# A new order of steps: four heads at a time, three level/angle buffers, six buffers of transposed tiles

## The chip, the cores and the metric

The kernel runs on one core of one Trainium2 chip. The metric is the device time of one execution in microseconds (us). Three runs of the kernel before gave 346.86 us as their median (345.96 to 346.95).

## The reference

All tensors are float32. B = 4 batches, H = 8 heads, S = 768 time steps, D = 48 channels of a head; the model width is 8 x 48 = 384. First a recurrence with a complex decay, whose real part is read out, then a gated convolution:

```python
mag = np.sqrt(a_re * a_re + a_im * a_im)
scale = np.minimum(mag, 0.999) / (mag + 1e-06)
a_re_n, a_im_n = (a_re * scale, a_im * scale)
for t in range(S):
    ar, ai = (a_re_n[:, :, t, :, None], a_im_n[:, :, t, :, None])
    new_re = ar * S_re - ai * S_im
    new_im = ar * S_im + ai * S_re
    kv = np.einsum('bhd,bhe->bhde', k[:, :, t], v[:, :, t])
    S_re, S_im = (new_re + kv, new_im)
    y[:, :, t] = np.einsum('bhd,bhde->bhe', q[:, :, t], S_re)
...
x = y.transpose(0, 2, 1, 3).reshape(B, S, H * D)
for k in range(5):
    gate_pre += conv_w[k][None, None, :] * xp[:, k:k + S, :]    # xp: x with four zero rows ahead
gate = 1.0 / (1.0 + np.exp(-gate_pre))
val = x @ w_val
out = gate * val @ w_out
```

## The kernel before

The recurrence is not stepped through. Logarithms of the decay's size (the level) and its angle are summed up along time; keys and queries are multiplied by the exponentials of the level, falling or rising, and by the cosine and sine of the angle, so that causal products of 96-wide rows (48 cosine and 48 sine parts) give what the recurrence gives. This is done in chunks of 128 time steps with a state that is carried between chunks on TensorE.

**Units.** `UNITS` (line 22) cuts the work into nine units u0 to u8, each (batch, first head, heads, half of the time, halves). u0 has two heads of batch 0, first half; u1 the other six; u2 is batch 0, second half, all eight heads; u3 and u4 are the halves of batch 1, u5 and u6 of batch 2, u7 and u8 of batch 3. A half has three chunks of 128 steps. A unit's heads are taken in groups of two pairs, four heads (line 85; u0 has one group of two heads, u1 a group of four and one of two). `chunks` (lines 86 to 92) lists (unit, chunk, group): with `GROUPWISE = False` each chunk runs through its groups before the next chunk comes, with `True` each group runs through the three chunks of the half before the next group comes. The generators for scores, masks, states, state copies, outputs and output copies all go by this list.

**Steps.** `ORDER` (lines 31 to 44) is one string; each letter advances one generator by one step (table `streams`, lines 772 to 783; loop 784 to 785). Every step's instructions on TensorE, DVE and ACT are tied to the one before on the same engine by `turn` (line 114), so the string fixes the order on these three engines. SyncE issues the DMAs; its queue is not tied by `turn` (`PIN_SP = False`), the DMAs stand in it as they are emitted. The letters:

- A loads the inputs of a unit (`load`, 149); V loads a batch's v, and then in a step of its own moves the first 64 rows of each chunk, for all heads of a unit, to the lower and upper half of `v_lo` (`load_vl`, 182), a single constant tile; L and w load and convert the weights.
- a to p make level and angle of a unit in the tile `main` (`p_ln`, 344, takes the buffer): a logarithm and exponential on ACT; b, g, h, i, k, m on DVE; c, d, e, f on both; j and l a small product on TensorE (335) for the sum over the 128 partitions; n and o absolute value and sines on ACT into `qx`; p two exponentials on ACT.
- q makes the keys `kx` on DVE (two products, lines 448 and 450), r the queries in `qx` (the same lines). `kx` has one buffer.
- N moves a chunk of keys by DMA from `kx` to `kn` (`move_keys`, 190; lines 201 to 206), where rows are time steps.
- T flips a head's keys or queries: three transposes on TensorE (500) into a PSUM tile `mm`; U copies it on ACT to a tile `kT` or `qT` (508), each of the two kinds with `BUFS['kT']` buffers. Flips go group by group: four heads of keys, then the same four of queries.
- s scores (530) into one of two PSUM tiles; M masks them on DVE (542) into `sm`; t adds keys times values into the one state in PSUM, `S_ps` (564); u copies the four heads' part of it on ACT (579) to `S_sb`, or `S_cr` when the next half needs it; y outputs (601 from the state of the chunk before, 606 and 611 from `sm` with v and `v_lo`); v copies them on ACT (622) to `y_sb`; X collects rows of `y_sb` by DMA into `xT` (646).
- C and D are the two sides of the convolution on DVE (first tap 657, four more 660), G the gate's sigmoid on ACT (679), P values on TensorE (691), Z gate times value on DVE (715), O projections on TensorE (698), Q row copies on ACT to `ot` (728), W stores (734). E is a guard that checks sums for overflow.

**Waits.** Besides the fixed order an instruction waits for its data and for its buffer: a tile of a pool with n buffers can be written when the tile n earlier has been read for the last time. `BUFS` (line 26) holds these counts.

**Tables.** ACT's functions lie in three sets (line 49). `act` (132 to 136) puts a table load (134) ahead of an instruction whose sets do not hold the one loaded last; so the count of loads follows from the order of the letters alone.

Of the kernel before, what the change touches and what calls it, by code (L numbers as in the profile page):

```python
# [21 lines left out]
UNITS = ((0, 0, 2, 0, 1), (0, 1, 6, 0, 1), (0, 0, 8, 1, 1), (1, 0, 8, 0, 1), (1, 0, 8, 1, 1), (2, 0, 8, 0, 1), (2, 0, 8, 1, 1), (3, 0, 8, 0, 1), (3, 0, 8, 1, 1))  # L22
PIECES = ((0, 0, 384), (0, 384, 384), (1, 0, 384), (1, 384, 384), (2, 0, 384), (2, 384, 384), (3, 0, 384), (3, 384, 384))
CONVS = ((0, 0, 384), (0, 384, 384), (1, 0, 384), (1, 384, 384), (2, 0, 384), (2, 384, 384), (3, 0, 384), (3, 384, 384))
GROUPWISE = False
BUFS = {'in': 4, 'v': 2, 'kn': 2, 'xT': 2, 'z': 3, 'main': 2, 'tmp': 1, 'qx': 2, 'kx': 1, 'kT': 9, 'S': 1, 'S_sb': 2, 'S_cr': 4, 'y_sb': 4, 'sm': 2, 'ot': 2, 'mm': 4}
YSLOTS = 2
XSTEP = 2
PIN_SP = False
POOLQ = ''  # L30
ORDER = (
    "AAaaAVbccAaeLfAagLiLiblVmdchwAhwjVdkkwhnwohowjwwwkpkpqcrqAnrTwwNaTeTUwfTUgUNUasiiMlbyomsvsoMNwcMwdwA"
    "htphAjAuqpVyckAVtvkuwyrqAtnvurTNwaTNUTwUTeaTNTbfUwUTUTUTgUTUTUTUisUUicwlMscmysvwXMowysdMMXoshAetvAwt"
    "hsuwuypyMtMtpqjvkAvfrkAuuyqnyvtvXtuurTgaTNTTUiUNTUiTUClUCUNTamTTXtUtbUTUTXuTUCXTUTCUATUTACUtUDsUCusD"
    "cCtDPcCDCPDGCGZGMdZyMhyvesvshMjMoykoyksvvsnMPMuuoyoZyvXOvXpOXQqpOWqXQfWAQWDTrNDTUTrUDTNUTCTUDTUTCUTU"
    "NDTUTDUTCAUTUDVTUTCUTDUVtUCtUDsuuaDtMtsgaAsPbGiAGPGZciMdlZymyvsvhPMhpMyZpqyvsrqvAusAucttujurNMTaTkTN"
    "UyUkUTvMTNnTeTAyUUUTvTUTUTUXTUTUTUTUXTUtUtUsuXuatMtyfbsvsgOAXMoiMcCyiQDlCvWdDymosshvDuOhDCpDjCOQkpWk"
    "cPrqnCPAQqWAGPGZNZrToCNTMTCUyMoNCyevsUvUCXuMtCXyGutZvVtuTTUVTUTUTXTUTUTUTUXTUTUTUTUtUsUsMyMfsyMvsvga"
    "yMsAviuyaMiyDvbulvXtmctAsuXDpOCDCupqOQrqcWAOQAWrNDTQTCUTWTUDTUNDTUCTUTDUTUCTNUTDUTUMTUDTUTUDTaeytAUt"
    "UsUvsuMXuatMyXbyvftsAvgsPMGMGCGDcyZDyvCuDsvCusdMDydMDyvCXhPvCVCGhGhXjZPhkcXejXPZfkknOkZOnDDQDWODQWDD"  # L40
    "gPQWDCoPZDoCDPoDCoCPCCCPCGGZZCOiGGZZiOQiWilQlWmOmpOQqpWqOpQpWOqNQWETrQNTrrUTTUTUTUWTUTNUTUTUTUTUTUTU"
    "TUTUsUqUtsutturTNMTMUTTNTyyvNsvsMtMyyvusvusMUUTMUTUTTyyUUUTUTTUTUTUTUTUsUUtMvsvXusMXysMvXsttuXyuyMvC"
    "sMvDtCtuDyuCDyvMtDvEuXEDyCXPvCCCXGCPGZXCCPZGDDCPDZDCODDGZDOQCWDCODQCWDGGPQWPZZOOQWOQWQW"
)
TURN = 2.0 ** 24
RADIAN = 2.0 * PI / 2.0 ** 32 * (1.0 - 2.0 ** -22)
# [6 lines left out]
def kernel(  # L53
# [34 lines left out]
        for rs, n in (  # L88
            [(rs, n) for rs in groups[u] for n in range(f0 * HN, (f0 + nf) * HN)] if GROUPWISE
            else [(rs, n) for n in range(f0 * HN, (f0 + nf) * HN) for rs in groups[u]]  # L90
# [53 lines left out]
    def dma(key, **kw):  # L144
        pool = key in POOLQ
        ins = (nc.gpsimd if pool else nc.sync).dma_start(**kw)  # L146
        return turn("sp", ins) if PIN_SP and not pool else ins

    def load(u, nm):
        b, h0, g, f0, nf = units[u]  # L150
        t = sb.tile([P, g, nf, JH, D], F32, name=f"{nm}_in", tag="in", bufs=BUFS["in"])
        src = {"ar": a_re, "ai": a_im, "k": k, "q": q}[nm][b, :, f0 * HS:(f0 + nf) * HS]
# [11 lines left out]
    def load_v(u):  # L164
        b, h0, g, f0, nf = units[u]
        if h0 == 0:
            v_b[b] = sb.tile([C, H, NCH, D], F32, name="v_in", bufs=BUFS["v"])
        for hs in halves_of(u):
# [5 lines left out]
    def halves_of(u):  # L174
        b, h0, g, f0, nf = units[u]
        if g == H:
            return [slice(0, H)]
        return [slice(w * (H // 2) + h0, w * (H // 2) + h0 + g // 2) for w in range(2)]
# [11 lines left out]
    def move_keys(u, n):  # L190
        b, h0, g, f0, nf = units[u]
        if n % HN == 0:
            tl[u]["kn"] = sb.tile([C, HN, g * C2 + 32], F32, name="kn", bufs=BUFS["kn"])
            nc.gpsimd.memset(tl[u]["kn"][:, :, g * C2:], 0.0)
# [15 lines left out]
    def load_raw(src):  # L210
        raw = sb.tile([P, NT * (EXT + S)], F32, name="raw", tag="xT", bufs=BUFS["xT"])
        raws.append(raw[:, :NT * DM * 2].bitcast(I64))
        dma("L",
            out=raws[-1].rearrange("p (c o) -> p c o", c=NT), in_=src.rearrange("(c p) o -> p c o", p=P)
        )

    def load_cw():
        raws.append(sb.tile([TAPS * NT, P], I64, name="raw_cw", tag="ot", bufs=BUFS["ot"]))
        dma("L", out=raws[-1], in_=conv_w.rearrange("t (c p) -> (t c) p", p=P))
# [44 lines left out]
    def mm():  # L264
        return ps.tile([P, 512], F32, name="mm", bufs=BUFS["mm"])

# [669 lines left out]
```

## Time and profile before

| | |
|---|---|
| median of three runs | 346.86 us (345.96 to 346.95) |
| the profiled execution | 347.51 us |
| its span, first to last instruction | 345.7 us |
| mean granted TensorE clock, share of full speed | 0.959 |
| instructions | 8663 |

The profile is one execution. Busy time of an engine counts its instructions; a share of the span says nothing of which engine is late at a given time, so the sections on the chain of waits, the timelines and the windows are read beside it. Times are microseconds from the start of the span; "idle before" is how long an engine stood still ahead of an instruction and what ended that. DVE is VectorE, ACT is ScalarE, PE is TensorE, SPq is SyncE's DMA queue. L500 is line 500 of the kernel before.

### The profile page before, as it was taken

The numbers are of one execution on the slowest core, as the hardware profiler recorded it, in microseconds if no ns is written. First come the engines' busy times: TensorE is split into PE (matmuls) and PEld (weight loads), VectorE is DVE, ScalarE is ACT, GpSimd is POOL, SyncE is SP. The second block draws the span as 40 slices with busy tenths as digits, with TensorE's granted clock in tenths as the row PEclk, the third lists the DMA queues.
The fourth block names the chain that finished last, engine by engine and source line by source line (L and its number), as shares of the span: only waits on it lengthen the run. The fifth ranks groups of instructions, "written<-read, shape, count | busy, mean of one in ns | idle before, by whom it ended". The sixth has DMA issues, their size and how long they took to land.

```text
span 345.7 us, 8663 instructions
## 1 busy us (share of the span) xinstructions
PE 278.2 (80%) x3591; PEld 212.4 (61%) x3591; DVE 251.0 (73%) x349; ACT 234.0 (68%) x423; POOL 6.2 (2%) x30
## 2 busy tenths in 40 slices
PE   0375676669994698798979979899999887999993
PEld 0153565558672586586749965777555577896551
DVE  4798979996925977927995179969998946148920
ACT  6989689768783596588974967868595751824121
POOL 5000000000000000000000000000000000000000
PEclk9999999889999699989995999999999999999999
DMA  7995997456017876764074947763311343221112
GB/s 196 354 227 164 234 219 200 132 138 176 24 43 141 241 195 138 203 168 130 31 204 127 193 118 212 232 179 76 91 43 46 108 122 99 44 72 40 52 50 73
DMA packets 58184, 47.83 MB, mean 138 GB/s; under 512 B 9758, under 2 KB 53803, under 8 KB 58139
## 3 DMA queue, kind: packets, MB, share of 16 engines
q1 hardware_dynamic: 58138, 47.21, 53.6%
q8 instruction: 30, 0.49, 0.6%
q14 instruction: 16, 0.12, 0.1%
HBM read 25.97 MB, written 4.72 MB: 89 GB/s over the span
## 4 chain that ended last, share of the span: by engine, by line
PE 47%; DVE 21%; ACT 11%; issue 8%; DMA 7%; SPq 4%; DVEq 0%; ACTq 0%
PE mm L698 10%; PE mm L691 9%; PE mm L500 8%; PE sc_ps L530 5%; SPq L146 4%; PE y_ps L601 4%; DVE z L660 4%; DVE kx L450 4%; PE S_ps L564 3%; ACT main L136 3%; DVE qx L450 3%; PE mm L335 3%; PE y_ps L611 3%; PE y_ps L606 3%; DMA ar_in<-in_a_re_dram 2%
## 5 line engine op out<-in xcount | busy, mean ns | idle before, releaser
L660 DVE SCALAR_TENSOR_TENSOR z<-xT,cw_sb,z 128x384 f32<-128x384 f32 x96 | 55.2, 612 | 0.8
L542 DVE TENSOR_TENSOR sm<-sc_ps,mask 128x384 f32<-128x384 f32 (+1 forms) x51 | 26.6, 530 | 39.3 <-PE sc_ps L530 33.3
L691 PE MATMUL mm<-xT,w_sb 128*128 128x384 f32 x144 | 49.4, 492 | 0.3 <-DMA xT<-y_sb 0.3
L698 PE MATMUL mm<-w_sb,z 128*128 128x384 f32 x144 | 48.5, 489 | 0.0
L530 PE MATMUL sc_ps<-qT,kT 96*64 96x64 f32 x1152 | 43.4, 230 | 3.3 <-ACT qT L139 1.4
L530 PEld LDWEIGHTS sc_ps<-qT,kT 96*64 96x64 f32 x1152 | 39.6, 144 | 5.5 <-issue 2.5
L500 PE MATMUL mm<-ident,kx 128*96 128x128 f32 x192 | 29.0, 302 | 15.3 <-DVE kx L450 9.2
L500 PE MATMUL mm<-ident,qx 128*96 128x128 f32 x192 | 31.0, 317 | 11.6 <-DVE qx L450 6.3
L139 ACT COPY y_sb<-y_ps 112x256 f32<-112x256 f32 (+1 forms) x51 | 17.1, 364 | 33.6 <-PE y_ps L611 33.6
L136 ACT ACTIVATE main<-main 128x1152 f32<-128x1152 f32 (+2 forms) x36 | 38.1, 1061 | 0.6 <-DVE main L419 0.3
L698 PEld LDWEIGHTS mm<-w_sb,z 128*128 128x128 f32 x144 | 27.0, 190 | 18.3
L691 PEld LDWEIGHTS mm<-xT,w_sb 128*128 128x128 f32 x144 | 26.7, 190 | 18.3 <-DMA xT<-y_sb 0.8
L500 PEld LDWEIGHTS mm<-ident,kx 128*96 128x96 f32 x192 | 23.1, 140 | 19.8 <-issue 7.4
L500 PEld LDWEIGHTS mm<-ident,qx 128*96 128x96 f32 x192 | 24.1, 145 | 16.4 <-ACT kT L139 9.5
L139 ACT COPY qT<-mm 96x384 f32<-96x384 f32 x64 | 27.3, 507 | 7.0 <-PE mm L500 6.0
L134 ACT ACT_TABLE_LOAD x24 | 30.8, 1283 | 1.2 <-PEq L920 0.8
L139 ACT COPY ot<-mm 128x384 f32<-128x384 f32 x24 | 11.4, 475 | 27.1 <-PE mm L698 17.2
L139 ACT COPY kT<-mm 96x384 f32<-96x384 f32 x64 | 26.9, 490 | 3.0 <-PE mm L500 2.9
L601 PE MATMUL y_ps<-qT,S_sb 96*48 96x128 f32 x256 | 23.4, 303 | 6.6 <-ACT S_sb L139 4.8
L564 PE MATMUL S_ps<-v_in,kn 128*64 128x48 f32 x640 | 26.4, 236 | 0.9 <-DMA kn<-kx 0.5
L606 PE MATMUL y_ps<-sm,v_in 128*48 128x64 f32 x384 | 21.9, 235 | 5.5 <-DVE sm L542 5.5
L564 PEld LDWEIGHTS S_ps<-v_in,kn 128*64 128x64 f32 x640 | 23.9, 153 | 3.2 <-ACT S_sb L139 1.2
(75 smaller groups left out, 394.2 us busy)
## 6 DMA issues: line engine op xcount, KB each, us to landing
kn<-kx SPq DMA_DIRECT2D x21, 378.0 KB
out_dram<-ot SPq DMA_DIRECT2D x24, 192.0 KB
ar_in<-in_a_re_dram SPq DMA_DIRECT2D x7, 576.0 KB
ai_in<-in_a_im_dram SPq DMA_DIRECT2D x7, 576.0 KB
k_in<-in_k_dram SPq DMA_DIRECT2D x7, 576.0 KB
q_in<-in_q_dram SPq DMA_DIRECT2D x7, 576.0 KB
xT<-y_sb SPq DMA_DIRECT2D x48, 72.0 KB
v_lo<-v_in SPq DMA_DIRECT2D x6, 288.0 KB
```

The source lines that it names most:

```text
L134: turn("act", nc.scalar.preload_act_table_set(sets[0]))
L136: return turn("act", nc.scalar.activation(*args, **kw))
L139: return turn("act", nc.scalar.copy(out, in_))
L500: pe(nc.tensor.transpose(pt[:C2, j, :], src[:, j, f, h, :], ident))
L530: pe(nc.tensor.matmul(o[w * HC:(w + 1) * HC, c * HC:(c + 1) * HC], part(u, 0, h, n, key, key + HC), part(u, 1, h, n, query, query + HC), s ...
L542: dve(nc.vector.tensor_tensor(out=t, in0=sc_ps[i % 2][:, :len(rs) * 3 * HC].rearrange("p (r x) -> p r x", x=3 * HC), in1=mask[:, None, :]. ...
L564: pe(nc.tensor.matmul(S_ps[b][c:c + 64, head(u, h) * D:(head(u, h) + 1) * D], kn[:, n % HN, at:at + 64], v_b[b][:, head(u, h), n], start=( ...
L601: pe(nc.tensor.matmul(to(r, w, 0, C), S_of[b, head(u, h), n - 1], part(u, 1, h, n), start=(r == 0), stop=False, skip_group_check=True,))
L606: pe(nc.tensor.matmul(to(r, w, HC, C), v_b[b][:, head(u, h), n], sm[:, r, (1 + w) * HC:(2 + w) * HC], start=(n == 0 and r == 0), stop=Fals ...
L660: dve(nc.vector.scalar_tensor_tensor(out=z, in0=xT[:, c, EXT + t0 - t:EXT + t0 - t + n], scalar=cw_sb[:, TAPS - 1 - t, c:c + 1], in1=z, op ...
L691: pe(nc.tensor.matmul(pv[:, :n], wv_sb[:, ci, c * P:(c + 1) * P], xT[:, ci, EXT + t0:EXT + t0 + n], start=(ci == 0), stop=(ci == NT - 1),))
L698: pe(nc.tensor.matmul(po[:, :DM], z[:, ci, m:m + P], wo_sb[:, ci, :], start=(ci == 0), stop=(ci == NT - 1)))
```

## The change

`GROUPWISE` becomes `True`: a group of four heads goes through the three chunks of its half before the next group starts. `BUFS` has three level/angle tiles `main` (two before), six transposed tiles of each kind (nine), three `S_sb` (two) and three `y_sb` (four). `ORDER` is replaced as a whole. It holds the same letters as often as before, so the same steps are done; by the rule of lines 132 to 136 it gives 28 table loads where the old one gives 24.

```diff
--- before.py
+++ after.py
@@ -22,25 +22,25 @@
 UNITS = ((0, 0, 2, 0, 1), (0, 1, 6, 0, 1), (0, 0, 8, 1, 1), (1, 0, 8, 0, 1), (1, 0, 8, 1, 1), (2, 0, 8, 0, 1), (2, 0, 8, 1, 1), (3, 0, 8, 0, 1), (3, 0, 8, 1, 1))
 PIECES = ((0, 0, 384), (0, 384, 384), (1, 0, 384), (1, 384, 384), (2, 0, 384), (2, 384, 384), (3, 0, 384), (3, 384, 384))
 CONVS = ((0, 0, 384), (0, 384, 384), (1, 0, 384), (1, 384, 384), (2, 0, 384), (2, 384, 384), (3, 0, 384), (3, 384, 384))
-GROUPWISE = False
-BUFS = {'in': 4, 'v': 2, 'kn': 2, 'xT': 2, 'z': 3, 'main': 2, 'tmp': 1, 'qx': 2, 'kx': 1, 'kT': 9, 'S': 1, 'S_sb': 2, 'S_cr': 4, 'y_sb': 4, 'sm': 2, 'ot': 2, 'mm': 4}
+GROUPWISE = True
+BUFS = {'in': 4, 'v': 2, 'kn': 2, 'xT': 2, 'z': 3, 'main': 3, 'tmp': 1, 'qx': 2, 'kx': 1, 'kT': 6, 'S': 1, 'S_sb': 3, 'S_cr': 4, 'y_sb': 3, 'sm': 2, 'ot': 2, 'mm': 4}
 YSLOTS = 2
 XSTEP = 2
 PIN_SP = False
 POOLQ = ''
 ORDER = (
-    "AAaaAVbccAaeLfAagLiLiblVmdchwAhwjVdkkwhnwohowjwwwkpkpqcrqAnrTwwNaTeTUwfTUgUNUasiiMlbyomsvsoMNwcMwdwA"
-    "htphAjAuqpVyckAVtvkuwyrqAtnvurTNwaTNUTwUTeaTNTbfUwUTUTUTgUTUTUTUisUUicwlMscmysvwXMowysdMMXoshAetvAwt"
-    "hsuwuypyMtMtpqjvkAvfrkAuuyqnyvtvXtuurTgaTNTTUiUNTUiTUClUCUNTamTTXtUtbUTUTXuTUCXTUTCUATUTACUtUDsUCusD"
-    "cCtDPcCDCPDGCGZGMdZyMhyvesvshMjMoykoyksvvsnMPMuuoyoZyvXOvXpOXQqpOWqXQfWAQWDTrNDTUTrUDTNUTCTUDTUTCUTU"
-    "NDTUTDUTCAUTUDVTUTCUTDUVtUCtUDsuuaDtMtsgaAsPbGiAGPGZciMdlZymyvsvhPMhpMyZpqyvsrqvAusAucttujurNMTaTkTN"
-    "UyUkUTvMTNnTeTAyUUUTvTUTUTUXTUTUTUTUXTUtUtUsuXuatMtyfbsvsgOAXMoiMcCyiQDlCvWdDymosshvDuOhDCpDjCOQkpWk"
-    "cPrqnCPAQqWAGPGZNZrToCNTMTCUyMoNCyevsUvUCXuMtCXyGutZvVtuTTUVTUTUTXTUTUTUTUXTUTUTUTUtUsUsMyMfsyMvsvga"
-    "yMsAviuyaMiyDvbulvXtmctAsuXDpOCDCupqOQrqcWAOQAWrNDTQTCUTWTUDTUNDTUCTUTDUTUCTNUTDUTUMTUDTUTUDTaeytAUt"
-    "UsUvsuMXuatMyXbyvftsAvgsPMGMGCGDcyZDyvCuDsvCusdMDydMDyvCXhPvCVCGhGhXjZPhkcXejXPZfkknOkZOnDDQDWODQWDD"
-    "gPQWDCoPZDoCDPoDCoCPCCCPCGGZZCOiGGZZiOQiWilQlWmOmpOQqpWqOpQpWOqNQWETrQNTrrUTTUTUTUWTUTNUTUTUTUTUTUTU"
-    "TUTUsUqUtsutturTNMTMUTTNTyyvNsvsMtMyyvusvusMUUTMUTUTTyyUUUTUTTUTUTUTUTUsUUtMvsvXusMXysMvXsttuXyuyMvC"
-    "sMvDtCtuDyuCDyvMtDvEuXEDyCXPvCCCXGCPGZXCCPZGDDCPDZDCODDGZDOQCWDCODQCWDGGPQWPZZOOQWOQWQW"
+    "AAaaALbcAcLaeLfAagVwiwiwbldmAchwhwjdkwhwhwkjwwnowokcwpkqneAaqwfTNTUNgaiUNipblVtmcVrucwtAuArtwAeTuTUw"
+    "fUgssVidiVMolhMhojmwsakyyvaMkywvnbvpXXwpqcrAcqAAAedTNTUNhTorTUUNUhoTwjUwTTfkTUUgTUpTTiTsUiUksUUMtnMs"
+    "qsplqAyuatyvuvtmaNtTTNMTUTUMrsUsUyNuuwbtAyAvMvMXuycrttyvuXuvtctwTXuTuUTeTUTUTUTUXTfssMUagtAsyaMiyMUi"
+    "UTvCTvCTUTUDPCuDCdDPCoCDCyoDCUhUPCvhXCbXGjGGsZcZsMldMZsmOhpkOQqpWhOAQqcWjQyWrNyvMNTvrTUTUyNUvtVkukXn"
+    "tueTXTUTUTkVfTTAtAUtgUTUATUTUiTuTuisDCsMotCsMoCyyDMUUCTUTDUlCvvPDunmoDtDyuDoDUDUPDvXXGPGZGZsZpsMOMaq"
+    "pOqAQpWOQrpWNrasNyyQvWTvMTNUTqUTUTATUATUbTUTTycAAtvUXUTUTUTquTXcssttMNdMsruyUUyhUUMNvrTvTuTTtyaCNDUC"
+    "UTADUTUACTvTDaXsCsDXuCtDuCtMCsGMyGCUUCTUTMUTCvTbyGyveAutUVtUhUjVUvTukXTuTsksXfMtMsagyyUMUUiTvTiUTvPu"
+    "acPZbnctZyDuDUCUDPvCXDeXdlsZomsoOMMDDOQCWDCDfOCDQphWsDhyQqpjWPMAvkPqGGGPZNZkTNTZUTUrTUONUnrAAOQAWgoT"
+    "TTiQyUiWUyvolTvmTUXUtUsucsXMtMdsyuhyMvCyvDCtvDTuXCTUTDUTXCUTTUDTUPCUUDCCPGCGZCCPpZhpqjOckqsQWstGMuTN"
+    "ZsUMNykryvNTvMTUrTUOUnOQeWfTTTtQgyUWUuTUViTUTiUTUTlvXTmsosXMtMosyDUyDUMUTvDTvTCUPDuCDDpPCDCpDyqtUtDU"
+    "vPquXuXsGDsNMtZyMuNsCvyEGMGNZtvyZurEvTTXUETrUTUOUXTQCTUTWDUTDUTTUDTUTUDTTDsCsMCtyMuCyvCCsGCGtMUtUCTU"
+    "TUCPvCuuGyZtUPUvuXXPZsZsMyMyvsvOMyQWOvXOXQWDOQDWDDPQDWDGDPDZDDPCCCOCCGGOZQZWOQWOQWOQWQW"
 )
 TURN = 2.0 ** 24
 RADIAN = 2.0 * PI / 2.0 ** 32 * (1.0 - 2.0 ** -22)
```

## Rows read from the trace of the kernel before

**Rows 1.** Page, part 1: busy us, share of span, instructions of each engine

```profile
PE 278.2 (80%) x3591; PEld 212.4 (61%) x3591; DVE 251.0 (73%) x349; ACT 234.0 (68%) x423; POOL 6.2 (2%) x30
```

**Rows 2.** Page, part 4: the chain that ended last, by engine

```profile
PE 47%; DVE 21%; ACT 11%; issue 8%; DMA 7%; SPq 4%; DVEq 0%; ACTq 0%
```

**Rows 3.** Windows: us; busy PE, PEld, DVE, ACT, POOL (instructions); PEclk, DMA share, GB/s

```profile
0.00:286.15 286.15, 227.15 (x2845) 173.43 (x2845) 223.45 (x299) 214.58 (x374) 6.22 (x30) 0.95 0.61 154
286.15:345.70 59.55, 51.06 (x746) 39.02 (x746) 27.57 (x50) 19.44 (x49) 0.00 (x0) 0.99 0.23 62
```

**Rows 4.** Timeline, DVE: start, us, line, out<-in, count, [idle before <-what ended it]

```profile
82.56 0.42 DVE L657 TENSOR_SCALAR z<-xT,cw_sb 128x384 f32<-128x384 f32 x1 [2.91 <-DMA xT<-y_sb]
...
103.67 1.36 DVE L448 TENSOR_TENSOR main<-main,k_in 128x1152 f32<-128x1152 f32 x1 [4.63 <-ACT main L136]
...
111.66 0.42 DVE L657 TENSOR_SCALAR z<-xT,cw_sb 128x384 f32<-128x384 f32 x1 [4.04 <-DMA xT<-y_sb]
...
155.60 0.56 DVE L542 TENSOR_TENSOR sm<-sc_ps,mask 128x384 f32<-128x384 f32 x1 [6.67 <-PE sc_ps L530]
...
196.73 1.26 DVE L542 TENSOR_TENSOR sm<-sc_ps,mask 128x384 f32<-128x384 f32 x2 [8.39 <-PE sc_ps L530]
...
283.56 2.56 DVE L450 TENSOR_TENSOR kx<-qx,main 128x2304 f32<-128x2304 f32 x1 [4.57 <-DMA kn<-kx]
```

**Rows 5.** Page, part 5: a group's count, busy us and mean ns

```profile
L134 ACT ACT_TABLE_LOAD x24 | 30.8, 1283 | 1.2 <-PEq L920 0.8
```

**Rows 6.** Timeline, ACT, at four places

```profile
8.24 1.28 ACT L134 ACT_TABLE_LOAD   x1
9.54 0.44 ACT L136 ACTIVATE main<-main 128x288 f32<-128x288 f32 x1
...
113.85 0.48 ACT L139 COPY ot<-mm 128x384 f32<-128x384 f32 x1 [7.17 <-DMA out_dram<-ot]
...
153.03 1.67 ACT L139 COPY qT<-mm 96x384 f32<-96x384 f32 x4
```

**Rows 7.** Windows around the first masks of u4 and u5

```profile
140.00:160.00 20.00, 16.65 (x282) 14.02 (x279) 12.43 (x11) 15.04 (x31) 0.36 (x2) 0.91 0.65 174
180.00:200.00 20.00, 18.06 (x320) 16.89 (x320) 8.72 (x15) 12.69 (x28) 0.00 (x0) 0.74 0.73 156
```

**Rows 8.** Timeline, SyncE's DMA queue: start and length of issuing

```profile
123.86 1.65 SPq L146 DMA_DIRECT2D v_lo<-v_in  x2
...
272.09 1.61 SPq L146 DMA_DIRECT2D kn<-kx  x2
...
278.70 15.00 SPq L146 DMA_DIRECT2D kn<-kx  x9
```

**Rows 9.** Chain that ended last, in order of time: start, us, engine, tile, line

```profile
119.12 3.18 DVE z L660 x6
```

**Rows 10.** Timeline, PE, the output that reads u3's v_lo

```profile
132.78 0.37 PE L611 MATMUL y_ps<-sm,v_lo 128*48 128x64 f32 x5 [0.63 <-DMA v_lo<-v_in]
```

**Rows 11.** Timeline, PE, outputs that waited for a state copy

```profile
65.13 1.10 PE L601 MATMUL y_ps<-qT,S_sb 96*48 96x128 f32 x8 [2.70 <-ACT S_sb L139]
...
308.10 0.64 PE L601 MATMUL y_ps<-qT,S_cr 96*48 96x128 f32 x8 [0.41 <-ACT S_cr L139]
```

**Rows 12.** Timeline, PE, from u8's queries to the end

```profile
290.22 1.57 PE L530 MATMUL sc_ps<-qT,kT 96*64 96x64 f32 x48
291.62 0.62 PE L564 MATMUL S_ps<-v_in,kn 128*64 128x48 f32 x16
292.07 0.61 PE L601 MATMUL y_ps<-qT,S_sb 96*48 96x128 f32 x8
...
293.85 1.57 PE L530 MATMUL sc_ps<-qT,kT 96*64 96x64 f32 x48
...
330.27 4.03 PE L691 MATMUL mm<-xT,w_sb 128*128 128x384 f32 x12
334.14 5.97 PE L698 MATMUL mm<-w_sb,z 128*128 128x384 f32 x18
```

## The prediction

> **What bounds the kernel now.** I read the engine totals first: TensorE is busy 278.2 us of 345.7, VectorE (DVE) 251.0, ScalarE (ACT) 234.0 [rows 1]. No engine fills the span. The chain that ended last says the same: 47% lies on TensorE, 21% on DVE, 11% on ACT, and the rest is hand-offs and DMA [rows 2]. So the loss is waiting between engines that take turns at being late, and a change that only reorders steps can matter.
>
> Then I cut the span at one mark: 286.15 us, where the key pass (kx) of the last unit, u8, has ended and its query pass begins. The table by windows gives two stages of different kinds [rows 3]. In stage 1 (0 to 286.15) DVE works 223.5 us and ACT 214.6; what counts there is how long DVE stands still, 286.15 - 223.45 = 62.7 us. In stage 2 (59.55 us) TensorE works 51.1 and DVE only 27.6: it is bound by TensorE, whose last matmuls end at 334.14 + 5.97 = 340.1, 5.6 us ahead of the end [rows 12]; a copy and a store follow.
>
> The large DVE waits of stage 1 I took from its timeline: 6.67 before a mask of u4, 8.39 before one of u5, 4.57 for the DMA that moves u7's keys, 2.91 and 4.04 for the collecting DMAs ahead of a convolution, and 4.63 for an exponential, which I expect to come again elsewhere and leave out of the sum [rows 4].
>
> **The change part by part.** The work is the same, but for table loads; only steps move, and three buffer counts and the order of chunks with them. So I count the letters of both orders ahead of and behind the mark and price them by rows. Prices, as the spacing of neighbours where there is one. TensorE: twelve of the large matmuls of lines 691 and 698 take 334.14 - 330.27 = 3.87, so a step of six 1.94; two scores 291.62 - 290.22 = 1.40, so 0.70 each; a state 292.07 - 291.62 = 0.45; an output half of 293.85 - 292.07, 0.89 [rows 12]. DVE: a tap 0.53 (six in 3.18) [rows 9]; a wide product 1.36, the key and query passes 2.56, a mask 0.56, of which the next pass covers some 0.08 [rows 4]. ACT: a copy of a flipped tile 0.4 (four in 1.67) [rows 6].
>
> *Stage 1, DVE work moved past the mark:* two taps (1.1), three gate products (1.4, priced as masks, whose size they have), the guard (0.6, about a mask) and u8's query product (1.35) go behind it, three masks of u7 (1.4) come ahead: -3.0 us.
>
> *Four heads at a time.* Now all eight heads of a half must be flipped and copied (16 flips, 14 to 16 copies ahead of the first scores of units 2 to 8) before its scores run; DVE's 6.67 and 8.39 end on those scores. In the new order 9 to 14 flips and 9 or 10 copies stand ahead of them, so 4 to 6 copies of 0.4, about 2 us, fall out of each burst; and with a third level/angle buffer u5's keys are made right behind u4's queries, so DVE has 14 us of other work between u5's queries and its first mask instead of a few. But TensorE was busy through those waits: 16.7 and 18.1 us of 20 [rows 7]. What it still has to do is not saved. Between nothing and the whole 15.1 I take half, -7.5, since about half of each burst is removed.
>
> *The key buffer (still one).* u8's kx waited 4.57 for u7's moves, whose DMAs stood between stores in SP's queue from 272.09 to beyond 278.70 [rows 4, 8]. In the new order those moves are issued at steps 899 to 910 and kx follows at 1002, some 20 us of DVE work later: -4.6, hidden by that work.
>
> *Collects ahead of convolutions.* A convolution's first tap stood a median 19 steps behind its last collect, in the worst case ahead of it; now 34, at least 5. The queue behind such a tap on DVE is the query product of u3, and ACT's row copy of the same stretch waited 7.17 for a store that stood behind collects in SP's queue, with u3's flips behind it [rows 6]. Of 2.91 + 4.04 I take 4.0 and count ACT's 7.17 no second time, as it overlaps: between 0 and -7.
>
> *Table loads.* By the rule of lines 132 to 136 the old order gives the 24 loads of the trace [rows 5], the new one 28: 4 x 1.28 = 5.1 us on ACT. ACT stands still for 286.15 - 214.58 = 71.6 us of stage 1 [rows 3], so some are hidden: 0 to +5.1, I take +2.6. A load runs from 8.24 to 9.52 and the pass behind it starts at 9.54, so nothing is added after it [rows 6].
> The Trainium skill, "ScalarE: Activation LUTs", section "What ACT_TABLE_LOAD costs", puts about 1.38 us of draining on top of each load, 2.66 us a switch. That speaks against an order with four more; by it the four cost an estimated 10.7 and, half hidden, 5.3, and the sum below would be some 2.7 us higher. The gap of 0.02 us in the row contradicts the added drain, so I keep the row.
>
> *New close distances.* Two waits are made tighter. u5's kx (step 559) now follows u4's moves (512 to 526) and u4's last key flip (556), instead of 100 steps behind; u7's moves in the old order needed 283.56 - 272.09 = 11.5 us from the first issue [rows 4, 8], and the new order has about 7 us of DVE work for that: up to +4.4. Queued behind it are u4's masks. And the second half of the v rows (v_lo) for u5 is issued only when u4's outputs are done, 27 steps ahead of its use, 5.5 us of TensorE work; for u3 the DMA went out from 123.86 to 125.5 and the matmul that reads it still waited at 132.78 [rows 8, 10], 7.3 us after the last issue: up to +3. Between 0 and +7.4 I take +4.
>
> *Stage 2.* Behind the mark the old order has on TensorE 16 flips, 11 scores, 10 states, 12 outputs and 12 large products; the new one 16, 9, 6, 9 and 16: it leaves four projections of earlier rows as filler and has less of u7 to do. 4 x 1.94 - 2 x 0.70 - 4 x 0.45 - 3 x 0.89 = +1.9, in a stage without cover; I write +2.0.
>
> **Sum.** -3.0 - 7.5 - 4.6 - 4.0 + 2.6 + 4.0 + 2.0 = -10.5. The profiled execution took 347.5 us (span 345.7 and 1.8 around it), 0.7 above the median 346.86; so 347.5 - 10.5 = 337.0, on the scale of the median **336.5**.
>
> A cross-check without any wait: I cut both orders in pieces of 50 steps, added up each engine's work in a piece by the trace's durations, and summed the busiest engine's share over the pieces: 304 before, 298 after, so 6 us better balanced; in pieces of 200 steps, 284 and 286. It supports a gain of a few us but no large one.
>
> **The rivals.**
> *TensorE was the late one in the bursts.* Then DVE's 6.67 and 8.39 were idle time of an engine off the path, and nothing is saved there, nor at the collects, where ACT's flips ran behind. Left: -3.0 - 4.6 + 2.6 + 4.0 + 2.0 = +1.0, so 347.9. For it: TensorE's 18.1 of 20 us around u5, in which it was at the lower clock level for part (granted 0.74) [rows 7]. Against it: at a low clock because it had waited before; a smoother order would win that back too.
> *The state's copies come onto the path (slower).* With four heads through all three chunks, the state of chunk n+1 adds into the PSUM columns that chunk n's copy still reads, and no other group's state stands between; the output of n+1 needs that copy too. A copy is short but stands in ACT's one queue behind table loads of 1.28 us and wide passes. The old order shows the price: an output waited 0.41 for such a copy at 308.10, 2.70 at 65.13 [rows 11]. Of some 34 such pairs, at about 1 us when ACT is busy, 11 exposed ones eat my whole gain; with half exposed, 347.5 - 10.5 + 17 = 354. Against it: the new order leaves a median of 7 steps between a state and its copy (6 before), and S_sb has a third buffer.
> *All of it works.* The bursts, collects and moves vanish whole and the new distances hold: -3.0 - 15.1 - 4.6 - 7.0 + 1.0 + 0 + 2.0 = -26.7, so 321.
> *It doesn't do what it says:* 13 of u5's 16 flips still stand ahead of its first score, so four heads at a time could pay nothing at u5. That is the first rival at one place, and lies within its time.
>
> **How the numbers follow.** Forecast (330 to 343): 0.48. All works (321): 0.14. TensorE late (about 348): 0.14, of which most is within 0.3%, what a measurement of this kernel can just tell from no change. State copies or another new wait (354): 0.24. Faster: 0.48 + 0.14 and a little of the third, 0.63; same 0.11; slower 0.26. The range, 324 to 353, leaves out about half of each outer case (0.07 and 0.12).
>
> **What would show it.** DVE waits ahead of the first masks of u4 and u5 under 4 us each; no wait of kx on its DMA at u8; no tap waiting over 2 us on a collect; 28 table loads of 1.28 us; from the end of u8's key pass to the end about 61 us; that pass ending near 274. I am wrong if outputs wait for S_sb copies by more than some 12 us in total, if kx of u5 waits over 4 us, if v_lo stalls the outputs at u5 or u7, or if TensorE's granted clock falls in more slices than now.

## The result and the profile after

The changed kernel takes **326.54 us** (median of four runs, 325.34 to 328.29) against 346.41 us before (four runs, 345.80 to 346.95): the ratio is 0.9431, with a 95% interval of 0.9378 to 0.9484. The forecast was 336.5 with a range of 324 to 353: the sign and the range held, but the gain is 19.9 us where 10.4 were forecast, nearly twice as much. The profiled execution has a span of 323.8 us (345.7 before). Beside the first four experiments the kernel before ran from 340.43 to 349.68, and since the ratio there is taken to the six fastest of its seventeen runs, the medians of all runs stand beside it.

The page of the changed kernel: busy time by engine, the chain that ended last, and the group of table loads.

```profile
PE 268.7 (83%) x3591; PEld 204.0 (63%) x3591; DVE 249.7 (77%) x349; ACT 237.6 (73%) x427; POOL 6.7 (2%) x30
...
PE 55%; ACT 15%; DMA 12%; DVE 9%; SPq 4%; issue 3%; DVEq 0%; ACTq 0%
...
L134 ACT ACT_TABLE_LOAD x28 | 35.9, 1283 | 1.3 <-PEq L920 0.8
```

The numbers of matmuls and of DVE's passes are those of [rows 1], and there are four table loads more than in [rows 5]. The chain lies on TensorE for 55% instead of 47%, on VectorE for 9% instead of 21% [rows 2]: DVE has mostly left the path.

The windows, cut as in [rows 3] where u8's key pass ends (now 259.27 us):

```profile
0.00:259.27 259.27, 212.06 (x2925) 162.52 (x2925) 218.37 (x293) 217.78 (x378) 6.72 (x30) 0.97 0.66 168
259.27:323.80 64.53, 56.68 (x667) 41.49 (x666) 31.35 (x57) 19.81 (x50) 0.00 (x0) 0.95 0.23 67
```

Stage 1 is 26.9 us shorter, stage 2 is 5.0 longer. In the forecast's own account, DVE's idle time in stage 1 went from 62.7 us to 259.27 - 218.37 = 40.9, so 21.8 less, and 5.1 us less of its work lies ahead of the mark (3.0 were forecast); that is the 26.9.

A second account, by TensorE, says more. It stood still for 345.7 - 278.2 = 67.5 us before and 323.8 - 268.7 = 55.1 now, 12.4 less; and the same 3591 matmuls were busy 9.5 us less. Together that is the whole 21.9 by which the span is shorter; it says where the time went, not why. Windows of 60 us show the stretches that changed (behind the length stand the busy times of PE, PEld, DVE, ACT and POOL, then the granted clock, the DMA share and GB/s), first of the kernel before:

```profile
60.00:120.00 60.00, 45.33 (x587) 35.33 (x583) 44.74 (x57) 41.46 (x75) 0.36 (x2) 0.89 0.50 125
...
180.00:240.00 60.00, 53.56 (x928) 45.32 (x929) 43.06 (x65) 42.04 (x87) 0.36 (x2) 0.91 0.64 160
```

and of the changed one:

```profile
60.00:120.00 60.00, 54.68 (x925) 44.63 (x923) 52.19 (x67) 51.30 (x96) 0.47 (x3) 0.97 0.56 150
...
180.00:240.00 60.00, 59.07 (x669) 42.44 (x668) 53.33 (x72) 48.53 (x81) 0.70 (x3) 1.00 0.43 115
```

TensorE is busy 59.07 of 60 us in the second of them, at a granted clock of 1.00, the level of 2.4 GHz. Before, it ran part of this stretch, 180.8 to 191.1, at a granted 0.50, the level of 1.2 GHz, after standing still for 2.15 us ahead of 181.45. It starts with less than before: 25.18 us of work in the first 60 instead of 31.35. From there to u8's key pass it stands still for 12.4 us where it stood still for 30.4.

The clock accounts for about half of the 9.5. In the stretches at a granted 0.50 TensorE was busy 22.9 us before (64.8 to 68.2, 75.0 to 78.4, 112.6 to 119.4, 146.7 to 150.1, 180.8 to 191.1) and is busy 13.5 us now (44.4 to 58.1, 109.3 to 112.7, 276.5 to 280.0). If the same work takes half as long at the upper level, that is an estimated 4.7 us. What made the rest, at the upper level, shorter is not shown.

The groups by line say which waits of TensorE went (idle before a group and its releasers at the end of the row), before:

```profile
L500 PE MATMUL mm<-ident,qx 128*96 128x128 f32 x192 | 31.0, 317 | 11.6 <-DVE qx L450 6.3 <-ACT kT L139 5.3
...
L601 PE MATMUL y_ps<-qT,S_sb 96*48 96x128 f32 x256 | 23.4, 303 | 6.6 <-ACT S_sb L139 4.8 <-issue 1.7
```

and after:

```profile
L500 PE MATMUL mm<-ident,qx 128*96 128x128 f32 x192 | 28.7, 295 | 1.5 <-ACT kT L139 1.5
...
L564 PE MATMUL S_ps<-v_in,kn 128*64 128x48 f32 x640 | 26.5, 229 | 10.5 <-DMA kn<-kx 7.9 <-ACT S_sb L139 2.5
...
L601 PE MATMUL y_ps<-qT,S_sb 96*48 96x128 f32 x256 | 20.9, 280 | 1.5 <-ACT y_sb L139 1.5
```

The flips of queries and the outputs hardly wait any more, 15.2 us less; 9.6 of it come back as states (0.9 before) that wait above all for moved keys.

DVE's waits, summed by what it waited for (us, times, the longest), before:

```profile
DVE sm L542 <- PE sc_ps L530: 33.3, 14, 8.4
...
DVE z L657 <- DMA xT<-y_sb: 7.2, 3, 4.0
```

and after:

```profile
DVE z L657 <- DMA xT<-y_sb: 8.6, 4, 5.0
...
DVE sm L542 <- PE sc_ps L530: 6.5, 6, 2.2
DVE kx L450 <- DMA kn<-kx: 5.0, 1, 5.0
```

Up to the mark alone, the stage that the forecast counts by DVE, the waits of masks for scores fell from 22.3 to 3.2 and those of taps for collected rows from 7.2 to 0.2; nearly all of the 8.6 that taps wait now lies in stage 2. A key pass waits 5.0 instead of 4.6, in another place. The waits for ACT at lines 374 and 386 rose from 5.2 to 11.7: the exponential that the forecast left out of its sum did come again elsewhere.

### The profile page after: what moved, and what is told of

Its sections match the earlier page's. It is cut to its first block, busy times and chain, and to the rows that moved or that the text cites. A ratio compares the mean times of both kernels' runs of the same rounds, so it can differ in the third digit from the quotient of the medians.

```text
span 323.8 us, 8672 instructions
## 1 busy us (share of the span) xinstructions
PE 268.7 (83%) x3591; PEld 204.0 (63%) x3591; DVE 249.7 (77%) x349; ACT 237.6 (73%) x427; POOL 6.7 (2%) x30
## 4 chain that ended last, share of the span: by engine, by line
PE 55%; ACT 15%; DMA 12%; DVE 9%; SPq 4%; issue 3%; DVEq 0%; ACTq 0%
PE mm L698 13%; PE mm L691 12%; PE sc_ps L530 8%; PE mm L500 6%; DMA ar_in<-in_a_re_dram 5%; SPq L146 4%; PE y_ps L601 4%; PE S_ps L564 3%; PE mm L335 3%; ACT main L136 3%; DMA kn<-kx 3%; PE y_ps L606 3%; PE y_ps L611 3%; ACT L134 2%; DMA v_lo<-v_in 2%
## 5 line engine op out<-in xcount | busy, mean ns | idle before, releaser
L530 PEld LDWEIGHTS sc_ps<-qT,kT 96*64 96x64 f32 x1152 | 38.4, 142 | 12.3 <-issue 6.5
L500 PE MATMUL mm<-ident,kx 128*96 128x128 f32 x192 | 28.1, 293 | 14.9 <-DVE kx L450 12.9
L564 PE MATMUL S_ps<-v_in,kn 128*64 128x48 f32 x640 | 26.5, 229 | 10.5 <-DMA kn<-kx 7.9
L500 PEld LDWEIGHTS mm<-ident,kx 128*96 128x96 f32 x192 | 21.7, 134 | 18.7 <-issue 13.7
L564 PEld LDWEIGHTS S_ps<-v_in,kn 128*64 128x64 f32 x640 | 23.1, 144 | 14.3 <-ACT S_sb L139 5.8
L500 PE MATMUL mm<-ident,qx 128*96 128x128 f32 x192 | 28.7, 295 | 1.5 <-ACT kT L139 1.5
L500 PEld LDWEIGHTS mm<-ident,qx 128*96 128x96 f32 x192 | 22.5, 136 | 6.1 <-ACT kT L139 2.0
L139 ACT COPY ot<-mm 128x384 f32<-128x384 f32 x24 | 11.4, 474 | 18.2 <-PE mm L698 15.1
L450 DVE TENSOR_TENSOR kx<-qx,main 128x2304 f32<-128x2304 f32 (+2 forms) x9 | 20.6, 2288 | 5.1 <-DMA kn<-kx 5.0
L601 PE MATMUL y_ps<-qT,S_sb 96*48 96x128 f32 x256 | 20.9, 280 | 1.5 <-ACT y_sb L139 1.5
```

The lines of the kernel that those rows point to most:

```text
L139: return turn("act", nc.scalar.copy(out, in_))
L450: dve(nc.vector.tensor_tensor(out=dst, in0=tl[u]["qx"], in1=mj[:, s].rearrange("p j x d -> p (j x) d")[:, :, None, :].to_broadcast([P, JH ...
L500: pe(nc.tensor.transpose(pt[:C2, j, :], src[:, j, f, h, :], ident))
L530: pe(nc.tensor.matmul(o[w * HC:(w + 1) * HC, c * HC:(c + 1) * HC], part(u, 0, h, n, key, key + HC), part(u, 1, h, n, query, query + HC), s ...
L564: pe(nc.tensor.matmul(S_ps[b][c:c + 64, head(u, h) * D:(head(u, h) + 1) * D], kn[:, n % HN, at:at + 64], v_b[b][:, head(u, h), n], start=( ...
L601: pe(nc.tensor.matmul(to(r, w, 0, C), S_of[b, head(u, h), n - 1], part(u, 1, h, n), start=(r == 0), stop=False, skip_group_check=True,))
```

## The experiments

All ratios are to the kernel before, timed beside the run. Each diff shows only the piece of `ORDER`, `BUFS` or the code that changes; ends of strings and lines are cut.

**One part alone in the kernel before: o_four.** Chunks go by groups from u2 on. The letters at u5's first scores are shown; the other units are changed alike:

```diff
-            [(rs, n) for rs in groups[u] for n in range(f0 * HN, (f0 + nf) * HN)] if GROUPWISE
+            [(rs, n) for rs in groups[u] for n in range(f0 * HN, (f0 + nf) * HN)] if u >= 2
...
-TTUVTUTUTXTUTUTUTUXTUTUTUTUtUsUsMyMfsyMvsvga
+TTUVTUTUTXTUTUssMMTUTUXTUyTUTUsMTUtUUfyvsvga
```

> The kernel before with one part of the change alone: four heads at a time from u2 on. Ahead of a unit's first two scores stand 8 copies instead of 14 to 16; its scores, masks and outputs go group by group; buffers and the other steps stay. Forecast (half of DVE's 6.67 and 8.39 before the first masks of u4 and u5 is on the path): 7.5 less than before, about 339. If all of it is on the path, as in the case that all works: 15 less, about 331. If TensorE was the late one there: within 1 of before. If state copies come onto the path: slower than before, and outputs wait for them by more than 5 us in total.

Ratio 1.0751 (1.0643 to 1.0860), 368.96 us against 346.72 by the medians of all runs: **slower by 22 us**. In this kernel and in o_three the first output of u3 stands ahead of the step that moves v_lo's rows for its batch (it reads them at 125.54, the DMA is issued at 125.96), so this output uses the rows of the batch before; the numbers of matmuls, passes and copies are the same. DVE's first line of waits:

```profile
DVE sm L542 <- PE sc_ps L530: 46.6, 17, 9.3
```

The waits of masks rose from 33.3 to 46.6. A group's chunks follow each other through score, mask, state, state copy and output; with little else put between them each hand-over lies bare (this reading is argued from the order and the waits). Fewer copies ahead of the scores, 8 instead of 14 to 16, did not pay by themselves in this order. States waited 6.7 us for state copies (0.4 before), outputs 4.7 as before: the second rival's mechanism, though it is not the largest part. TensorE stood still for 8.3 us more and its same matmuls were busy for 12.8 us more; it was busy for 44.5 us at the lower clock level, 22.9 before. If the level halves the pace, that is an estimated 10.8 of the 21.1 us by which its span is longer.

**o_stall.** Two taps go behind u3's query passes, a row copy and its store behind the copies of u3's first flips.

```diff
-QfWAQWDTrNDTUTrUDTNUTCTUDTUTCUTUNDTU
+QfWATrNTUTrUDDDTNUTCTUDTUTCUTUQWNDTU
```

> The kernel before with the stall at u3 taken away (108 to 114 us): the two taps that stand ahead of u3's query passes go behind them, the third row copy and its store behind the copies of the first group's flips. Forecast: 4.0 was taken for both collecting waits together, 2.3 of it for this one, so about 344.5. If every engine stood still there and nothing made it good later: 5 to 6 less, about 341. If it is made good later: within 1 of before.

Ratio 1.0189 (1.0067 to 1.0312), by all runs 350.25 us against 346.72: no gain, rather a loss. Yet the stall is gone. Timeline of DVE (u3's query pass, 113.80 before) and of TensorE behind it:

```profile
106.84 2.56 DVE L450 TENSOR_TENSOR qx<-qx,main 128x2304 f32<-128x2304 f32 x1
```

```profile
199.33 1.10 PE L601 MATMUL y_ps<-qT,S_sb 96*48 96x128 f32 x8 [3.00 <-issue]
```

and the window behind that, here and in the kernel before:

```profile
200.00:210.00 10.00, 10.00 (x156) 8.65 (x153) 6.04 (x10) 6.00 (x13) 0.18 (x1) 0.74 0.28 76
```

```profile
200.00:210.00 10.00, 8.29 (x160) 6.68 (x161) 7.76 (x13) 7.11 (x14) 0.18 (x1) 1.00 0.38 101
```

u3's queries came 7.0 us earlier and u5's first mask still 3.5 (193.22 instead of 196.73). Then an output stood still for 3.0 us, for which the profile names nothing but "issue"; the lower clock level came behind it (0.74 instead of 1.00 in the window), but there is no more of it than before, only later (0.83 from 180 to 210 us in both). At u5's last mask nothing was left (221.40 against 221.18). The traced execution ends where the one before ends; why the timed runs were slower is not shown.

**o_key.** The three moves of u7 go one behind the other, ahead of two stores.

```diff
-OqNQWETrQNTrrUTTUTUTUWTUTNU
+OqNNNQWETrQTrrUTTUTUTUWTUTU
```

> The kernel before with the three moves of u7's keys issued one behind the other, ahead of two stores, so that kx of u8 no longer waits 4.57 us. Forecast: the whole 4.6 is saved, about 342. If TensorE, which went on with u7's flips and scores until 285 us, sets the end there: 1.3 at most, about 345.5, and the wait shows up again before the masks of u7.

Ratio 1.0060 (1.0012 to 1.0108), by all runs 345.76 us against 346.72: no gain clear of the scatter. SyncE's queue and the key pass of u8:

```profile
271.42 6.72 SPq L146 DMA_DIRECT2D kn<-kx  x7
```

```profile
282.13 2.56 DVE L450 TENSOR_TENSOR kx<-qx,main 128x2304 f32<-128x2304 f32 x1 [3.81 <-DMA out_dram<-ot]
```

The wait shrank from 4.57 to 3.81 only. The three moves are seven DMAs and take 6.72 us to issue even side by side, so taking the stores [rows 8] from between them won little. The profile puts the end of the wait down to a store, which the key pass does not need; which landing ended it is not shown.

**o_three.** The three edits together.

> The kernel before with the three edits together (four heads at a time from u2 on, the stall at u3, the moves of u7). Forecast: -7.5 - 2.3 - 4.6 = 14.4 less, about 332. If these three are all of what the changed kernel gains, it lies near 326.5; if the third level buffer and the rest of the order carry most of the gain, it lies above 338.

Ratio 1.0623 (1.0520 to 1.0726), 364.16 us. Not the sum of three gains, and nowhere near the changed kernel: the gain is not in these three places one by one. Yet it is 4.8 below o_four, so the two edits that won nothing in the kernel before do win something in that order (6.9 had been forecast for both).

**The other way round: n_main2.** The changed kernel with two level/angle buffers; the first logarithms of u2 to u6 go back by 15 to 89 steps, behind the pass that frees the buffer, that of u8 by 106, and steps that hang on them by as much as they must.

```diff
-'main': 3
+'main': 2
```

> The changed kernel with two level/angle buffers instead of three: each unit's first logarithm, and what hangs on it, goes back behind the last pass that reads the buffer; nothing else is moved, but the order then needs 33 table loads instead of 28. If the third buffer is what carries the gain: at least 7 more than the changed kernel, 334 or above. If it is not: only the five loads count, between nothing and 5 x 1.28 = 6.4 more, so 326.5 to 333, by the half that the forecast took 329.7.

Ratio 1.0756 (1.0702 to 1.0810), 373.0 us, **46.5 above the changed kernel**, of which the five loads can be 6.4 at most. TensorE's first line of waits and DVE's:

```profile
PE mm L335 <- DVE main L325: 25.6, 6, 11.8
```

```profile
DVE main L355 <- ACT main L136: 18.9, 6, 5.8
```

Without the third buffer the preparation of a unit can't run ahead in this order: its small product on TensorE (335) waits for DVE's additions, a pass of DVE (355) for ACT. The first of these waits is 3.9 us in the changed kernel, the second doesn't occur. The kernel before has two such buffers too and takes 346.41, so this order depends on the third one; what a third one alone would do for the old order was not run.

**n_flat.** As n_main2, and the chunks one by one.

```diff
-GROUPWISE = True
+GROUPWISE = False
-'main': 3 ... 'kT': 6 ... 'S_sb': 3 ... 'y_sb': 3
+'main': 2 ... 'kT': 9 ... 'S_sb': 2 ... 'y_sb': 4
```

> As n_main2, and the chunks again one by one through both groups, with the buffer counts of the kernel before; steps that would come too early for that go back as far as they must. So it differs from n_main2 in four heads at a time alone, and from the kernel before in the order alone. If four heads at a time carries the gain (forecast 7.5 in DVE's waits ahead of the first masks): 7 or more above n_main2. If it costs as much as it saves, as in the case of state copies on the path: within 2 of n_main2, or below it.

Ratio 1.1684 (1.1636 to 1.1732), 404.94 us, **32 above n_main2**. DVE's first line of waits:

```profile
DVE z L715 <- PE mm L691: 22.6, 7, 12.8
```

So a step back to chunks one by one costs a lot in this order, and masks (15.8 us) are not where most of it shows. It is not four heads at a time alone: the counts of S_sb, y_sb and the transposed tiles went back with it. Both kernels push steps back mechanically and were not put in order again, so 46.5 and 32 are rather bounds from above than prices of a part.

**n_tables.** The edit was to double nine table loads.

```diff
-            turn("act", nc.scalar.preload_act_table_set(sets[0]))
+            for _ in range(2 if sets[0] == TRIG else 1):
+                turn("act", nc.scalar.preload_act_table_set(sets[0]))
```

> The changed kernel with each load of the table for the sines done twice: 9 loads of 1.28 us more on ScalarE, 11.5 us of work, nothing else. By the forecast (half of a load is hidden): 5.8 more than the changed kernel, 332.3. If ScalarE stands on the path all through: 11.5 more, 338. If TensorE sets the pace and ScalarE has slack: less than 2 more. The Trainium skill, page ScalarE: Activation LUTs, section What ACT_TABLE_LOAD costs, puts 1.38 us of draining on top of each load: by it 24 us of work more, an estimate, so 338 to 350 by the first two cases.

Ratio 0.9450 (0.9412 to 0.9487), span of the profiled execution 327.5. But its group of loads reads:

```profile
L135 ACT ACT_TABLE_LOAD x28 | 35.9, 1283 | 1.3 <-PEq L921 0.8
```

28 and not 37: no second load of a table that is already there stands in the trace, and the number of instructions, 8672, is that of the changed kernel. So it is a repeat of the changed kernel and says nothing of what a load costs; it shows that the ratios of two sets of runs agree within 0.2%, and that single profiled executions of one program differ by 3.7 us. This longer execution had less of the lower clock level (TensorE busy 6.8 us in it, 13.5 in the other) and more waiting, so the clock alone does not order the times.

**n_tail.** Six taps go behind u8's first two masks.

```diff
-CTUTWDUTDUTTUDTUTUDTTDsCsMCtyMuCyvCCsGCGtMUtU
+CTUTWUTUTTUTUTUTTssMCtyMDDDDDCuCyvCCsGCGtMUtU
```

> The changed kernel with six taps of the last batch's convolution, which wait for a collecting DMA at 270 us and stand ahead of u8's first two masks, put behind these masks. If this wait is what made the last stage longer than forecast (TensorE stood still before 276.1 and ran at the lower clock until 280): 3 to 4 less than the changed kernel, about 323. If TensorE has enough other work behind and the taps are then missed by the gates: within 1 of it.

Ratio 0.9484 (0.9440 to 0.9528): no gain over the changed kernel's 0.9431. TensorE, and ACT ahead of it:

```profile
282.77 1.52 PE L500 MATMUL mm<-ident,qx 128*96 128x128 f32 x6 [3.21 <-ACT kT L139]
```

```profile
281.42 0.94 ACT L136 ACTIVATE z<-z 128x384 f32<-128x384 f32 x2 [3.06 <-DVE z L660]
```

The wait moved on: two gates on ACT now waited 3.06 for the late taps, the copies of flips stand behind the gates in ACT's one queue, and the next flips waited 3.21 for the copies.

**n_kxlate and n_both.** u5's key pass, and the first of its moves, goes behind u4's first two masks; in n_both the last stage is ordered anew as well, with the third mask among the taps and the gates behind the copies.

```diff
-TUTquTXcssttMNdMsr
+TUTuTXcssttMdMqNsr
```
```diff
-CTUTWDUTDUTTUDTUTUDTTDsCsMCtyMuCyvCCsGCGtMUtUCTUTUCPvCuuG
+CTUTWUTUTTUTUTUTTssMCtyMuCysvDDMDDDCCCCtUtUCTUTUCPvCuuGGG
```

> The changed kernel with the key pass of u5, which waits 5.02 us for u4's moves, put behind u4's first two masks (and the first of u5's moves behind it). If the close distance costs what its waits show (TensorE stood still 2.08 us for that mask): 2 less than the changed kernel, 324.5. If the wait is covered: within 1 of it.

> n_kxlate, and the last stage ordered anew: six taps of the last batch's first half behind u8's first two masks, the third mask among them, and the two gates, for which ScalarE kept TensorE's flips waiting in n_tail, behind the copies. If that was all that stood in n_tail's way: 3 less than n_kxlate, about 321.5 to 323.5. If TensorE's work behind 276 us sets the end whatever its order: within 1 of n_kxlate.

n_kxlate: 0.9496 (0.9446 to 0.9546), no gain. The wait of the key pass is gone, but masks now wait 10.6 us for scores instead of 6.5 and states 10.1 for moved keys instead of 7.9: taking this wait away wins nothing. n_both: 0.9417 (0.9369 to 0.9464), 325.92 us, 3.4 below n_kxlate by the medians, as expected, though the intervals touch, and no measurable step below the changed kernel (321.5 to 323.5 were expected). In its trace the last stage, from the end of the key pass (260.37 + 2.55) to the end at 323.60, has no gap of TensorE left and is 60.7 us long instead of 64.5; 3.7 us were lost again ahead of it, in a stretch whose steps are those of n_kxlate. n_both and n_kxlate, around u5:

```profile
176.00:188.00 12.00, 9.73 (x94) 7.41 (x94) 5.23 (x10) 7.42 (x15) 0.31 (x1) 0.86 0.70 139
```

```profile
176.00:188.00 12.00, 12.00 (x160) 8.63 (x156) 9.62 (x16) 11.74 (x20) 0.32 (x1) 1.00 0.59 130
```

and what TensorE waited for in n_both:

```profile
177.35 0.31 PE L611 MATMUL y_ps<-sm,v_lo 128*48 128x64 f32 x2 [1.44 <-DMA v_lo<-v_in]
178.58 0.37 PE L611 MATMUL y_ps<-sm,v_lo 128*48 128x64 f32 x5 [0.92 <-DMA v_lo<-v_in]
```

The v_lo rows landed late in this execution; TensorE stood still and then had the lower clock for a while. Whether that is chance or follows from the edits was not settled.

**n_pe and n_dve.** More work on one engine, in the changed kernel:

```diff
+            for _ in range(2 if u > 1 else 0):
+                pe(nc.tensor.matmul(sc_ps[i % 2][:, 3 * P:], ident, ident, start=True, stop=True))
```
```diff
+            if u > 1:
+                dve(nc.vector.tensor_tensor(out=spare, in0=spare, in1=spare, op=ALU.add))
```

> The changed kernel with two more matmuls of 128 columns behind each score from u2 on, 84 in all, written where nothing reads: 84 x 0.11 = 9.2 us of work more on TensorE (three such take 0.33). If TensorE sets the pace from 56 us on, where it stands still for hardly a microsecond at a time: 8 to 9 more, 335. If a wait on other engines sets it: 0 to 4 more.

> The changed kernel with one more small pass behind each mask from u2 on, 42 in all of 0.2 to 0.28 us: 8 to 11.5 us of work more on VectorE (the sums over a unit's rows show 0.24 for 96 columns). If VectorE has slack, as ScalarE showed: less than 2.5 more, below 329. If it shares the pace with TensorE, as my forecast had it, which counted VectorE's waits: 6 or more, 332 and above.

n_pe: 1.0035 (1.0000 to 1.0070), 348.47 us. Two added matmuls (two records each) in the timeline, and the output behind them:

```profile
209.55 0.71 PE L535 MATMUL sc_ps<-ident 128*128 128x128 f32 x4
210.19 0.43 PE L608 MATMUL y_ps<-sm,v_in 128*48 128x64 f32 x8
```

210.19 - 209.55 = 0.64 for two, 0.32 each and not 0.11: the price had been taken from transposes. 84 x 0.32 = 26.9 us were added, and the time rose by 21.9, **0.8 of it** (0.7 of the 30.4 us by which TensorE's busy time rose in the trace). n_dve: 0.9493 (0.9442 to 0.9544). DVE was busy 257.6 us, 7.9 more than the changed kernel; the time is 0.5 to 0.7% above the two sets of the changed kernel by the ratios, 1.5 to 2.2 us and inside the intervals, so **some 0.3 of it at most**. TensorE sets the pace of the changed kernel; DVE has slack. The same work was not added to the kernel before, so that its pace was set otherwise rests on its chain [rows 2] alone.

## Why the prediction was right, and where its size was wrong

The direction and the main mechanism, waits between engines that an order can remove, were right. The size was wrong mostly in stage 1: -12.5 forecast, -26.9 measured.

**Four heads at a time (-7.5): mis-sized, and the argument for the half failed.** The step said that TensorE was busy through DVE's waits of 6.67 and 8.39, and that what it still has to do is not saved. Both waits are gone, and with them most of the smaller ones, 7.3 us in eight waits, that the forecast put at nothing (22.3 to 3.2 in all). DVE's timeline at u4's and u5's first masks:

```profile
148.82 2.56 DVE L450 TENSOR_TENSOR kx<-qx,main 128x2304 f32<-128x2304 f32 x1 [5.02 <-DMA kn<-kx]
151.30 1.01 DVE L542 TENSOR_TENSOR sm<-sc_ps,mask 128x384 f32<-128x384 f32 x2
...
173.45 1.03 DVE L542 TENSOR_TENSOR sm<-sc_ps,mask 128x384 f32<-128x384 f32 x2
```

Ahead of u4's masks DVE still stands still, now for u5's keys (5.02), and TensorE for 2.08 with it. TensorE's busy time there was not a fixed amount: ahead of u4's and u5's first masks it was at the lower clock level for 3.4 and 10.3 us (0.91 and 0.74 in [rows 7]), busy 12.6 us of them, the second time after standing still. The prediction noted that against its first rival and gave it no term. Over the whole span the clock accounts for about 4.7 of the 9.5 us of busy time that vanished with no matmul less. By DVE's waits the whole 15.1 would have been the better choice; what four heads at a time is worth alone no run shows, as o_four lost 22 and n_flat goes back with three buffer counts as well.

**One part or the whole.** The forecast added the parts as if each could be had alone. o_four, o_stall and o_key show that none can in the kernel before: +22, no gain, no gain. n_main2 and n_flat show that the new order depends on its buffers and its grouping, and only bound what they are worth. What the change brings, by the windows, is that there is nearly always a matmul ready from 60 us on. That this comes of units prepared further ahead and of hand-overs that lie under other work is the reading that fits n_main2 and o_four; no run shows it by itself.

**The key buffer (-4.6): right in the trace, wrong as a saving.** u8's key pass no longer waits, but u5's waits 5.02. Neither gave a gain where it was tried: o_key left 3.81 of its wait, and n_kxlate removed the other one.

**Collects (-4.0): the waits moved.** In stage 1, where the term counts them, they went from 7.2 to 0.2, the whole of the 7 that bounded it. But taps wait 8.6 us in all against 7.2, now in stage 2 (2.27 at 270.36 and 5.00 at 298.73), where those from 270.36 on hold up TensorE (below); "no tap waiting over 2 us on a collect" did not hold. Taken away alone in the kernel before (o_stall), one of these waits gained nothing.

**Table loads (+2.6): left open.** 28 came, as counted. Their price wasn't measured. The gap behind a load is again nil, and ACT stood still for only 1.3 us ahead of all 28 together:

```profile
171.56 1.28 ACT L134 ACT_TABLE_LOAD   x1
172.86 1.26 ACT L136 ACTIVATE tmp<-main,b_inv 128x1152 f32<-128x1152 f32 x1
```

This speaks, as in the prediction, against the extra drain of the Trainium skill, "ScalarE: Activation LUTs", section "What ACT_TABLE_LOAD costs".

**New close distances (+4.0): the waits came, the cost did not.** kx of u5 waited 5.02, more than the 4.4 that bounded it, and the prediction had called over 4 a sign of being wrong; n_kxlate shows that taking it away gains nothing. v_lo cost TensorE 1.0 us at u5 here and 2.4 us, with a lower clock behind it, in n_both.

**Stage 2 (+2.0): +5.0, a miscount and an overlooked wait.** The letters behind the mark are not what TensorE had left: in the kernel before, one score and three states of these letters ran while DVE still made u8's keys, and the trace shows 10 scores and 7 states there, not 11 and 10. With these the forecast's prices give 4 x 1.94 - 0.70 - 0.45 - 3 x 0.89 = +3.9. The rest is a wait and the clock, less the gaps of the old order, some 2.9 us. The taps that wait for u7's collects stand in DVE's queue ahead of u8's first masks:

```profile
270.36 0.42 DVE L657 TENSOR_SCALAR z<-xT,cw_sb 128x384 f32<-128x384 f32 x1 [2.27 <-DMA xT<-y_sb]
271.93 0.42 DVE L657 TENSOR_SCALAR z<-xT,cw_sb 128x384 f32<-128x384 f32 x1 [1.15 <-DMA xT<-y_sb]
272.45 3.11 DVE L660 SCALAR_TENSOR_TENSOR z<-xT,cw_sb,z 128x384 f32<-128x384 f32 x5
275.48 0.55 DVE L542 TENSOR_TENSOR sm<-sc_ps,mask 128x384 f32<-128x384 f32 x1
```

and TensorE waits for that mask and is slower after it (1.50 for one score, where two took 1.57 in [rows 12]):

```profile
276.09 0.43 PE L606 MATMUL y_ps<-sm,v_in 128*48 128x64 f32 x8 [1.80 <-DVE sm L542]
...
278.29 1.50 PE L530 MATMUL sc_ps<-qT,kT 96*64 96x64 f32 x24
```

The prediction had counted the steps between a collect and its tap ("at least 5") and not asked who stands behind the tap. The lower level lasted from 276.5 to 280.0, an estimated 1.7 us lost, beside the 1.80 of waiting. With that order mended, n_both's last stage took 60.7. That this is close to the 61 of the forecast is in part luck: 3.9 more work and 2.9 of gaps that went.

**The rivals.** TensorE late in the bursts did not come true: DVE's waits went, and with them time that TensorE lost itself. State copies on the path did not either: outputs waited 4.8 us for them before and nothing now, states 2.5 instead of 0.4; in o_four the mechanism appears. "All works" (321) came nearer than the forecast: without stage 2 it holds -28.7, against -26.9 measured and -12.5 in the forecast; but in part that is luck, as it had no wait for u5's keys (5.02) and collects and keys gained nothing as savings of their own.

**Slips.** 346.86 - 10.5 is 336.4 and not 336.5, and 321 is on the scale of the profiled execution (320.2 on that of the median); neither matters. The cross-check without any wait, 6 us, supported a gain of a few us "but no large one"; it counts work only, and most of the gain was waiting and clock.

## What to carry to other kernels

Where no engine fills the span, keep an account on the engine that has the most work as well: how long it stands still, and what its work takes at the clock that it then gets. The waits of a pinned order could not be taken out one by one here: an edit made its local wait smaller or removed it, and another wait took its place or the time stayed as it was; so price an order as a whole, and for each wait that is moved ask who is queued behind the waiting instruction. Look into the trace of an experiment for the thing that was added before reading its time.

## What was not expected of the hardware

A transposing float32 matmul of 128 columns took 0.11 us at the full granted clock (twelve in 1.31, from 269.62 to 270.93 in the changed kernel), a plain float32 matmul of 128 columns 0.32 (two in 0.64, n_pe). One program's profiled executions differed by 3.7 us in span (the changed kernel and n_tables), while the ratios of two sets of its timed runs agreed within 0.2%. Two kernels with the same steps around u5 differed by 2.4 us there in the wait for a DMA (v_lo: nothing in n_kxlate, 1.44 + 0.92 in n_both).
